# First three groups of a gated recurrence and its two-layer network, ordered by pairs

## The chip, the cores and the metric

The kernel runs on one core of one Trainium2 chip. The metric is device time in microseconds (us) for one execution, and the median over the runs is compared. Engines are named as in the profile: PE is TensorE (PEld its weight loads), DVE is VectorE, ACT is ScalarE, POOL is GpSimd, SP is SyncE, which here only issues DMAs.

## The reference

Four inputs q, k, v, alpha of shape (4 batches, 8 heads, 768 steps, 48 features) go through a recurrence with a state of 48 x 48 per batch and head. Its result, as 3072 tokens of 384 features, goes through a layer of 2048 units with GELU and a second layer back to 384.

```python
for t in range(S):
    state = alpha[:, :, t, :, None] * state + einsum('bhd,bhe->bhde', k[:, :, t], v[:, :, t])
    y[:, :, t] = einsum('bhd,bhde->bhe', q[:, :, t], state)
x = y.transpose(0, 2, 1, 3).reshape(B * S, H * D)        # 3072 x 384
h = x @ w_in                                             # 384 x 2048
g = gelu_tanh(h)
out = g @ w_out                                          # 2048 x 384
```

## The kernel before

**Tiles and groups.** The 768 steps are cut into six chunks of 128. A group G0 to G5 is one chunk of all four batches, four tiles of 128 tokens; a pair is two tiles of a group. Pairs are called p0 and p1 (G0), p2 and p3 (G1), p4 and p5 (G2).

**One pair through the recurrence.** ACT takes Ln of alpha (`e_ln`, L121). PE makes running sums over the chunk (`e_cum`, L129, and the chunk's total, L131). ACT takes three exponentials of them (`e_exp`: b, L142; its inverse, L143; the total, L144), and DVE multiplies q and k by the first two (qp, L146; kp, L148). Then for each tile: `t_qk` transposes qp and kp on PE (L165) and copies them out of PSUM (L167; on ACT where `evict` is `nc.scalar.copy`, else on DVE); `attn` makes the scores (PE, L178) and masks them (two DVE operations, L181); `kv` makes the chunk's contribution to the state (PE, L192) and updates the state (DVE, L201 and L203; in G0 L203 alone); `y` makes the output from old state and masked scores (PE, L214 and L217; in G0 L217 alone) and ACT copies it out (x, L220). x is transposed into xT either by PE and a DVE copy (`t_x`, L229 and L230) or by a DMA from SP (L222).

**The two layers.** `layer1` is a list of 16 pieces, each three PE products (L239) and one GELU on ACT (L242). For a half group a piece is 256 columns wide, for a whole group 512. `layer2` is a list of pieces of four products (L254), four pieces to a tile; the last of a tile is followed by a DVE copy (ot, L258) and a DMA out from SP.

**PSUM.** Three names share the eight banks: `ca` (two banks, one buffer, for the sums and for the scores of one tile), `yk` (two buffers: transposes, kv, y and xT) and `ff` (four buffers: pieces of layer 1, sums of layer 2).

**What sets the order.** The order is written out by hand: each engine does its work in the order in which `run` issues it. `_merge(main, side, first, last)` spreads a list of side work between the pieces of a list of main work. ACT holds one set of function tables at a time: `act_set(LN_EXP_SET)` (L112) loads one with Ln and Exp; before an activation whose function is not in the set that is loaded, the build puts a load of its own, listed under the line of that activation (L121, L142, L242).

**Order before.** p0 goes through whole (L325 to L328), then eight pieces of layer 1 for its half group, p1 whole, and the rest of layer 1 for G0. Layer 2 of G0 is merged with p2 (L341, L342). Layer 1 of the first half of G1 is merged with Ln, Exp and scores of p3 in its last 30% (L343, L344). Layer 2 of that half is merged with the state of p3 and with Ln and Exp of p4 and p5 (L346, L347), layer 1 of the second half with the scores of p4 and p5. From G2 on a loop (L352) does a group at a time: layer 2 of the group before, merged with the state of this group, its xT by DMA, and Ln and Exp of the next group; then layer 1 (512 columns wide), merged with the scores of the next group.

**Loads.** POOL issues all loads but the first, in the order of the program: G0 by pairs, between them the weights, then G1 by pairs, then G2 whole. a, q and k have two buffers each, so that a load for G2 waits until G0's has been used, and G3's until G1's has.

## Time and profile before

| | us |
|---|---|
| median of 3 runs (lowest to highest) | 240.38 (239.75 to 241.97) |
| the profiled execution, whole | 241.77 |
| its span, first to last instruction | 240.0 |
| PE busy | 186.0 (78%) |
| ACT busy | 134.3 (56%) |
| DVE busy | 108.7 (45%) |
| POOL busy | 51.5 (21%) |

The mean clock granted to TensorE over the span is 0.927 of full speed. Times in the profile are counted from the start of the span. A row of the timeline gives start, duration, engine, line, operation, result and sources, count, and in brackets the idle time before it and what ended it. A row of a table by stretches gives, after the stretch and its length, the busy time of PE, PEld, DVE, ACT and POOL with the number of instructions in parentheses, the granted clock, the share of DMA and GB/s. A busy PE is not a PE at its peak, since its products are pipelined.

### The profile page before, as it was taken

The page shows a single profiled execution, that of the slowest core. Times are in us where ns is not written, and L with a number is a line of the kernel's source. Part 1 is how long each engine was busy: PE and PEld are TensorE (multiplying, and loading weights), DVE is VectorE, ACT ScalarE, POOL GpSimd, SP SyncE. Part 2 cuts the span into 40 slices and gives each one's busy share as a digit, 9 for nine tenths or more (in the row PEclk, how much of TensorE's full clock was granted, in tenths as well). Part 3 has the DMA queues.
Part 4 walks back from the last instruction along what each step waited for, and adds up shares of the span by engine and source line. Part 5 has one row for each costly group of instructions (what it writes and reads, how often), then busy time and mean ns, then how long its engine had stood idle before and what let it go on. Part 6 is the DMA issues. An engine that isn't in the chain of part 4 may idle for free.

```text
span 240.0 us, 3997 instructions
## 1 busy us (share of the span) xinstructions
PE 186.0 (78%) x1641; PEld 116.0 (48%) x1648; DVE 108.7 (45%) x213; ACT 134.3 (56%) x228; POOL 51.5 (21%) x47
## 2 busy tenths in 40 slices
PE   0368258997665387569946999899998999999992
PEld 0146136864444155347622556554565555654561
DVE  5361234004750267377890465866568565110020
ACT  3426736944239926986851567486764865219600
POOL 7965634322000370162216000000000000000000
PEclk9999855999979559999995899999999999999999
DMA  7999999999900199979999961320012200240011
GB/s 144 174 214 178 203 216 175 172 190 181 163 33 0 31 192 182 89 163 209 145 169 216 169 21 37 80 85 3 0 52 66 82 3 0 68 112 19 0 68 67
DMA packets 44339, 26.22 MB, mean 109 GB/s; under 512 B 34304, under 2 KB 40960, under 8 KB 44320
## 3 DMA queue, kind: packets, MB, share of 16 engines
q0 software_dynamic: 32144, 19.27, 61.9%
q1 hardware_dynamic: 12176, 6.69, 11.5%
q8 instruction: 13, 0.21, 0.4%
q14 instruction: 6, 0.05, 0.1%
HBM read 25.17 MB, written 4.72 MB: 125 GB/s over the span
## 4 chain that ended last, share of the span: by engine, by line
PE 59%; DVE 13%; ACT 13%; DMA 7%; issue 5%; POOL 1%; DVEq 0%; POOLq 0%; ACTq 0%
PE hT L239 25%; PE acc L254 21%; PE qkT_ps L165 5%; PE at L178 4%; DMA xT<-x 3%; DVE atm L181 3%; DVE kp L148 3%; DMA k<-in_k_dram 3%; DVE qkT L167 2%; DVE st L203 2%; ACT gT L242 2%; ACT b L142 2%; ACT qkT L167 2%; ACT L142 2%; ACT L121 2%
## 5 line engine op out<-in xcount | busy, mean ns | idle before, releaser
L239 PE MATMUL hT<-xT,w_in 128*128 128x256 bf16 (+1 forms) x377 | 76.3, 352 | 8.1 <-DMA xT<-x 4.2
L242 ACT ACTIVATE gT<-hT 128x256 bf16<-128x256 f32 (+1 forms) x128 | 60.0, 491 | 32.2 <-PE hT L239 30.2
L254 PE MATMUL acc<-w_out,gT 128*128 128x384 bf16 x384 | 68.3, 326 | 0.0
L239 PEld LDWEIGHTS <-w_in 128*128 128x128 bf16 x384 | 38.8, 106 | 33.1 <-issue 6.9
L254 PEld LDWEIGHTS <-gT 128*128 128x128 bf16 x384 | 35.0, 97 | 21.3
L181 DVE TENSOR_TENSOR atm<-at,ut 128x512 bf16<-128x512 f32 x48 | 30.9, 686 | 23.8 <-PE at L178 23.8
L146 DVE TENSOR_TENSOR qp<-q,b 128x768 bf16<-128x768 f32 x12 | 11.5, 958 | 46.2 <-ACT b L142 45.7
L220 ACT CAST x<-yps 128x384 bf16<-128x384 f32 x24 | 11.5, 479 | 32.9 <-PE yps L217 25.3
L258 DVE COPY ot<-acc 128x384 f32<-128x384 f32 x24 | 13.4, 557 | 34.6 <-PE acc L254 33.1
L129 PE MATMUL cum<-la,ut_h 128*128 128x384 f16 x24 | 7.7, 350 | 16.4 <-ACT la L121 16.4
L91 POOL DMA_DIRECT2D a<-in_alpha_dram x7 | 10.2, 1458 | 47.1 <-ACT la L121 41.6
L167 DVE COPY qkT<-qkT_ps 128x1024 bf16<-128x1024 bf16 x18 | 12.4, 690 | 16.7 <-PE qkT_ps L165 16.7
L178 PE MATMUL at<-qkT 64*128 64x128 bf16 x192 | 10.7, 239 | 7.0 <-ACT qkT L167 4.9
L165 PE MATMUL qkT_ps<-ident,qp 128*128 128x128 bf16 x96 | 10.9, 245 | 6.5 <-DVE qp L146 6.5
L142 ACT ACTIVATE b<-cum 128x768 bf16<-128x768 f32 x12 | 9.7, 811 | 8.9 <-PE cum L131 7.6
L91 POOL DMA_DIRECT2D q<-in_q_dram x8 | 11.5, 1436 | 12.7 <-DVE qp L146 9.2
L91 POOL DMA_DIRECT2D v<-in_v_dram x8 | 11.4, 1428 | 11.1 <-issue 4.7
L178 PEld LDWEIGHTS <-qkT 64*128 64x128 bf16 x192 | 6.1, 102 | 15.8 <-ACT qkT L167 6.6
L165 PEld LDWEIGHTS <-qp 128*128 128x128 bf16 x96 | 7.9, 109 | 11.4 <-DVE qp L146 7.5
L131 PEld LDWEIGHTS <-la 128*128 128x128 f16 x96 | 5.6, 100 | 16.1 <-issue 11.9
L242 ACT ACT_TABLE_LOAD x9 | 11.5, 1283 | 2.5 <-PE hT L239 2.4
L165 PE MATMUL qkT_ps<-ident,kp 128*128 128x128 bf16 x96 | 10.9, 246 | 2.2 <-DVE kp L148 2.2
(40 smaller groups left out, 168.8 us busy)
## 6 DMA issues: line engine op xcount, KB each, us to landing
out_dram<-ot SPq DMA_DIRECT2D x24, 192.0 KB, 2.0
a<-in_alpha_dram POOLq DMA_DIRECT2D x4, 768.0 KB, 9.1
q<-in_q_dram POOLq DMA_DIRECT2D x4, 768.0 KB, 9.7
k<-in_k_dram POOLq DMA_DIRECT2D x4, 768.0 KB, 13.0
q<-in_q_dram POOLq DMA_DIRECT2D x4, 384.0 KB, 12.6
k<-in_k_dram POOLq DMA_DIRECT2D x4, 384.0 KB, 13.4
w_in<-in_moe_w_in_dram POOLq DMA_DIRECT2D x4, 384.0 KB, 9.4
w_out<-in_moe_w_out_dram POOLq DMA_DIRECT2D x4, 384.0 KB, 14.5
```

The lines of the kernel that those rows point to most:

```text
L91: (eng or self.nc.gpsimd).dma_start(t[:, lo:hi].rearrange("t b h d -> t (b h) d"), src)
L142: nc.scalar.activation(b8, cum[:, :, 0:H * D], AF.Exp)
L146: nc.vector.tensor_tensor(qp[:, :, :, 0:D], u0["qpair"], b8.rearrange("t i (h d) -> t i h d", h=H), op=ALU.mult)
L165: nc.tensor.transpose(ps[:, j, p, :], s[:, 2 * p:2 * p + 2, :].rearrange("t h d -> t (h d)"), self.ident)
L167: (evict or nc.vector.tensor_copy)(t, ps)
L178: nc.tensor.matmul(at[:, o, p, :], kT[sl, p, :], qT[sl, p, :], start=True, stop=True)
L181: nc.vector.tensor_tensor(atm[:, o], at[:, o], self.ut[:, None, :].to_broadcast([C, H // 2, C]), op=ALU.mult)
L220: nc.scalar.copy(x, yps.rearrange("t h d -> t (h d)"))
L239: nc.tensor.matmul(h, self.w_in[:, j, nt * C:(nt + 1) * C], xT[:, j, lo:hi].rearrange("p g t -> p (g t)"), start=j == 0, stop=j == self.NK ...
L242: nc.scalar.activation(gT[:, nt, lo * C:hi * C], h, AF.Gelu_apprx_tanh)
L254: nc.tensor.matmul(acc[mt], gT[:, nt, mt * C:(mt + 1) * C], self.w_out[:, nt, :], start=nt == 0, stop=nt == self.NFT - 1)
L258: nc.vector.tensor_copy(ot, acc[mt])
```

## The change

The order of work up to the end of layer 1 of G2 is written anew; the loop now begins at G3.

- G2 too is done in halves: p4 and p5 each have their own layer 1 and xT by PE and DVE instead of a DMA.
- A function `chain` takes a pair from transposes to xT: both transposes first, one copied out by DVE and one by ACT, then score and kv of the first tile, of the second tile, and the two outputs; `fill(i)` puts other work at five places. For p0 the fill is `warm(n)`: n products of zeros, 512 columns wide. For p1 it is layer 1 of p0's half group, for p2 pieces of layer 2 of G0.
- `decays` gives two steps, the first with the table load and Ln, the second with sums and exponentials. No GELU is issued between the two steps of a pair.
- p3, p4 and p5 have their scores merged into layer 1 of the half group before, and state, xT and decays of the next pair lie between pieces of layer 2.
- The loop is entered with eleven of the sixteen pieces of layer 2 of G2 left, and with the scores of G3 done.
- a, q and k get three buffers, the rings for la, qp and kp four, ot six; G2 is loaded by pairs, and the loads of G3 are issued behind layer 2 of G1. A tile of zeros is filled on DVE.

```diff
--- before.py
+++ after.py
@@ -60,12 +60,13 @@
         self.ut = const.tile([C, C], BF16, name="ut")
         self.ident = const.tile([C, C], BF16, name="ident")
         self.ones = const.tile([C, 1], F16, name="ones")
+        self.zero = const.tile([C, 512], BF16, name="zero")
 
         self.w_in = const.tile([C, self.NKT, self.d_ff], BF16, name="w_in")
         self.w_out = const.tile([C, self.NFT, self.d_model], BF16, name="w_out")
         self.state = [[const.tile([C, H // 2, 2 * D], BF16, name=f"st{b}_{i}") for i in range(2)]
                       for b in range(B)]
-        self.NR = 3
+        self.NR = 4
         self.la_ring = [const.tile([C, 2, H, 64], F16, name=f"la{i}") for i in range(self.NR)]
         self.qp_ring = [const.tile([C, 2, H, 64], BF16, name=f"qp{i}") for i in range(self.NR)]
         self.kp_ring = [const.tile([C, 2, H, 64], BF16, name=f"kp{i}") for i in range(self.NR)]
@@ -84,7 +85,7 @@
         c = group[0][0]
         if (n, c) not in self.loaded:
             self.loaded[n, c] = self.ld.tile([C, len(group), H, D], BF16 if n == "v" else F32, tag=n,
-                                             bufs=3 if n == "v" else 2, name=n)
+                                             bufs=3, name=n)
         t = self.loaded[n, c]
         lo, hi = (0, len(group)) if part is None else (2 * part, 2 * part + 2)
         src = self.src[n][lo:hi].rearrange("b h s d -> s (b h) d")[c * C:(c + 1) * C]
@@ -232,16 +233,31 @@
 
     def layer1(self, xT, gT, lo=0, hi=4):
         nc, C = self.nc, self.C
-
-        def piece(nt):
-            h = self.ps.tile([C, (hi - lo) * C], F32, tag="ff", bufs=4, name="hT")
+        hs = {}
+
+        def mm(nt):
+            h = hs[nt] = self.ps.tile([C, (hi - lo) * C], F32, tag="ff", bufs=4, name="hT")
             for j in range(self.NKT):
                 nc.tensor.matmul(h, self.w_in[:, j, nt * C:(nt + 1) * C],
                                  xT[:, j, lo:hi].rearrange("p g t -> p (g t)"),
                                  start=j == 0, stop=j == self.NKT - 1)
-            nc.scalar.activation(gT[:, nt, lo * C:hi * C], h, AF.Gelu_apprx_tanh)
-
-        return [lambda nt=nt: piece(nt) for nt in range(self.NFT)]
+
+        def act(nt):
+            nc.scalar.activation(gT[:, nt, lo * C:hi * C], hs.pop(nt), AF.Gelu_apprx_tanh)
+
+        def piece(nt):
+            mm(nt)
+            act(nt)
+
+        pieces = [lambda nt=nt: piece(nt) for nt in range(self.NFT)]
+        self.mm, self.act = mm, act
+        return pieces
+
+    def warm(self, n):
+
+        ps = self.ps.tile([self.C, 512], F32, tag="ff", bufs=4, name="idle")
+        for _ in range(n):
+            self.nc.tensor.matmul(ps, self.zero[:, 0:self.C], self.zero, start=True, stop=True)
 
     def layer2(self, group, gT, by_part=False, lo=0, hi=4):
         nc, C = self.nc, self.C
@@ -254,7 +270,7 @@
                 nc.tensor.matmul(acc[mt], gT[:, nt, mt * C:(mt + 1) * C], self.w_out[:, nt, :],
                                  start=nt == 0, stop=nt == self.NFT - 1)
             if part == self.NFT // 4 - 1:
-                ot = self.wk.tile([C, self.d_model], F32, tag="ot", name="ot")
+                ot = self.wk.tile([C, self.d_model], F32, tag="ot", bufs=6, name="ot")
                 nc.vector.tensor_copy(ot, acc[mt])
                 c, b = group[mt]
                 r = b * self.S + c * C
@@ -272,6 +288,7 @@
         pairs = [[g[0:2], g[2:4]] for g in G]
         self.act_set(LN_EXP_SET)
         self.load("a", G[0], 0, nc.sync)
+        nc.vector.memset(self.zero, 0.0)
         for n in "qkv":
             self.load(n, G[0], 0)
             if n == "q":
@@ -279,9 +296,8 @@
             if n == "k":
                 make_identity(nc, self.ident)
         nc.vector.memset(self.ones, 1.0)
-        self.pads(self.la_ring)
-        self.pads(self.qp_ring)
-        self.pads(self.kp_ring)
+        for i in range(self.NR):
+            self.pads((self.la_ring[i], self.qp_ring[i], self.kp_ring[i]))
         nc.vector.tensor_copy(self.ut, self.ut_h)
         for b in range(self.B):
             for i in range(2):
@@ -294,62 +310,102 @@
             self.load_w_in(i)
         for i in range(4):
             self.load_w_out(i)
-        for i in range(2):
-            for n in "aqkv":
-                self.load(n, G[1], i)
-        for n in "aqkv":
-            self.load(n, G[2])
-
-        def ln_exp(p):
-            self.e_ln(p)
-            self.e_cum(p)
-            self.e_exp(p)
-
-        def scores(p, evict=None):
-            return [f for cb in p for f in (lambda cb=cb: self.t_qk(cb, evict), lambda cb=cb: self.attn(cb))]
+        for g in (1, 2):
+            for i in range(2):
+                for n in "aqkv":
+                    self.load(n, G[g], i)
+
+        def run(*fs):
+            for f in fs:
+                f()
+
+        def decays(p):
+
+            return [lambda: (self.act_set(LN_EXP_SET), self.e_ln(p)), lambda: (self.e_cum(p), self.e_exp(p))]
+
+        def scores(p):
+            return [f for cb in p for f in (lambda cb=cb: self.t_qk(cb), lambda cb=cb: self.attn(cb))]
 
         def state(p, xT, lo):
-            for i, cb in enumerate(p):
-                self.yk(cb, xT, lo + i, False)
-            for i, cb in enumerate(p):
-                self.t_x(cb, xT, lo + i)
+            return [lambda i=i, cb=cb: self.yk(cb, xT, lo + i, False) for i, cb in enumerate(p)] + \
+                   [lambda i=i, cb=cb: self.t_x(cb, xT, lo + i) for i, cb in enumerate(p)]
 
         def new():
             return (self.grp.tile([self.C, self.NKT, 4, self.C], BF16, tag="xT", name="xT"),
                     self.grp.tile([self.C, self.NFT, 4 * self.C], BF16, tag="gT", bufs=1, name="gT"))
 
-        copy = nc.scalar.copy
-
-        (p0, p1), (p2, p3) = pairs[0], pairs[1]
+        def chain(p, xT, lo, fill):
+
+            u, w = p
+            fill(0)
+            self.t_qk(u)
+            self.t_qk(w, nc.scalar.copy)
+            fill(1)
+            self.attn(u)
+            self.kv(u)
+            self.attn(w)
+            self.kv(w)
+            fill(2)
+            self.y(u, xT, lo, False)
+            fill(3)
+            self.y(w, xT, lo + 1, False)
+            self.t_x(u, xT, lo)
+            fill(4)
+            self.t_x(w, xT, lo + 1)
+
+
+        p0, p1, p2, p3, p4, p5 = [p for g in (0, 1, 2) for p in pairs[g]]
         xT, gT = new()
-        ln_exp(p0)
-        for f in scores(p0, copy):
-            f()
-        state(p0, xT, 0)
-        first = self.layer1(xT, gT, 0, 2)
-        for f in first[:8]:
-            f()
+        self.e_ln(p0)
+        self.warm(10)
+        self.e_cum(p0)
+        self.e_exp(p0)
+        chain(p0, xT, 0, lambda i: self.warm((10, 3, 5, 2, 2)[i]))
         self.act_set(LN_EXP_SET)
-        ln_exp(p1)
-        for f in scores(p1, copy):
-            f()
-        state(p1, xT, 2)
-        for f in first[8:] + self.layer1(xT, gT, 2, 4):
-            f()
+        self.e_ln(p1)
+        la = self.layer1(xT, gT, 0, 2)
+        mm, act = self.mm, self.act
+        mm(0)
+        mm(1)
+        self.e_cum(p1)
+        self.e_exp(p1)
+        act(0)
+        act(1)
+        fill = {0: la[2:6], 1: la[6:8], 2: la[8:11], 3: la[11:13], 4: la[13:16]}
+        chain(p1, xT, 2, lambda i: run(*fill[i]))
+        run(*self.layer1(xT, gT, 2, 4))
+        l2 = self.layer2(G[0], gT, True)
         xT1, gT1 = new()
-        self.act_set(LN_EXP_SET)
-        side = [lambda: ln_exp(p2)] + scores(p2, copy) + [lambda: state(p2, xT1, 0)]
-        _merge(self.layer2(G[0], gT, True), side, 0.5, 1.0)
-        side = [lambda: self.act_set(LN_EXP_SET), lambda: ln_exp(p3)] + scores(p3)
-        _merge(self.layer1(xT1, gT1, 0, 2), side, 0.7, 1.0)
+        run(*l2[:4])
+        run(decays(p2)[0], *l2[4:6])
+        run(decays(p2)[1], *l2[6:11])
+        fill = {0: [], 1: l2[11:13], 2: l2[13:15], 3: l2[15:16], 4: []}
+        chain(p2, xT1, 0, lambda i: run(*fill[i]))
+        run(*decays(p3))
+        lc = self.layer1(xT1, gT1, 0, 2)
+        _merge(lc, scores(p3), 0.3, 0.9)
+        run(*state(p3, xT1, 2)[:2], decays(p4)[0])
         l2 = self.layer2(G[1], gT1, False, 0, 2)
-        side = [lambda: state(p3, xT1, 2)] + [lambda p=p: ln_exp(p) for p in pairs[2]]
-        _merge(l2, side, 0.1, 1.0)
-        side = [f for p in pairs[2] for f in scores(p)]
-        _merge(self.layer1(xT1, gT1, 2, 4), side, 0.1, 1.0)
-        prev = self.layer2(G[1], gT1, False, 2, 4)
-
-        for g in range(2, len(G)):
+        run(*l2[:1], *state(p3, xT1, 2)[2:], *l2[1:3], decays(p4)[1], *l2[3:])
+        _merge(self.layer1(xT1, gT1, 2, 4), scores(p4), 0.1, 0.9)
+        xT2, gT2 = new()
+        run(*state(p4, xT2, 0)[:2], decays(p5)[0])
+        l2 = self.layer2(G[1], gT1, False, 2, 4)
+        run(*l2[:1], *state(p4, xT2, 0)[2:], *l2[1:3], decays(p5)[1], *l2[3:])
+        self.load("a", G[3])
+        self.load("q", G[3])
+        self.load("k", G[3])
+        self.load("v", G[3])
+        _merge(self.layer1(xT2, gT2, 0, 2), scores(p5), 0.1, 0.9)
+        run(*state(p5, xT2, 2)[:2])
+        l2 = self.layer2(G[2], gT2, False, 0, 2)
+        (la0, ce0), (la1, ce1) = [decays(p) for p in pairs[3]]
+        run(la0, lambda: self.e_ln(pairs[3][1]))
+        run(*l2[:1], *state(p5, xT2, 2)[2:], *l2[1:2], ce0, *l2[2:5], ce1)
+        _merge(self.layer1(xT2, gT2, 2, 4), [f for p in pairs[3] for f in scores(p)], 0.1, 1.0)
+        prev = l2[5:] + self.layer2(G[2], gT2, False, 2, 4)
+
+        for g in range(3, len(G)):
             more = g + 1 < len(G)
             xT, gT = new()
```

## The prediction

> **What bounds the kernel now.** I read the busy time by stretches first, cut where a piece of layer work begins or ends on PE. The rows are: pair p0; p1 and the first layer of G0; second layer of G0 with p2; first layer of half of G1 with p3; from there to the end of the first layer of G2; the state of G2's successor beside G2's second layer; and the rest.
>
> ```profile
> 0.00:19.48 19.48, 6.92 (x73) 4.84 (x74) 9.69 (x31) 7.71 (x10) 15.29 (x23) 1.00 1.17 175
> 19.48:48.00 28.52, 20.46 (x168) 15.62 (x168) 6.45 (x12) 18.80 (x42) 12.75 (x12) 0.76 1.39 191
> 48.00:69.34 21.34, 15.32 (x146) 9.45 (x144) 9.81 (x20) 7.27 (x11) 3.24 (x2) 0.98 1.09 159
> 69.34:89.20 19.86, 11.92 (x91) 8.15 (x90) 4.50 (x6) 15.30 (x26) 5.42 (x4) 0.68 0.31 60
> 89.20:144.75 55.55, 42.99 (x432) 26.75 (x431) 33.97 (x62) 35.83 (x61) 14.77 (x9) 0.94 1.26 150
> 144.75:159.41 14.66, 13.91 (x152) 9.26 (x149) 11.85 (x25) 9.14 (x15) 0.00 (x0) 1.00 0.28 69
> 159.41:240.00 80.59, 74.52 (x593) 41.88 (x595) 32.38 (x58) 40.26 (x67) 0.00 (x0) 1.00 0.14 43
> ```
>
> The first number after the stretch is its length, the second PE's busy time. Behind 144.75 PE is busy over nine tenths of the time: PE bounds there, and the change leaves that code alone. Ahead of it PE idles for a quarter to two thirds, and the granted clock is partly halved. So what can be won lies in the first 145 us, in handovers. The timeline shows the worst one, ACT in the fourth stretch:
>
> ```profile
> 75.17 1.28 ACT L112 ACT_TABLE_LOAD   x1
> 76.46 1.28 ACT L242 ACT_TABLE_LOAD   x1
> 78.16 1.28 ACT L121 ACT_TABLE_LOAD   x1
> 80.31 1.28 ACT L142 ACT_TABLE_LOAD   x1
> 83.21 1.28 ACT L242 ACT_TABLE_LOAD   x1
> ```
>
> Five table loads in ten microseconds: a GELU stands between the explicit load and Ln, so Ln and then Exp load tables of their own. In the next stretch the state of G2 goes through xT by DMA, which PE waits for at its end:
>
> ```profile
> 128.03 0.59 PE L239 MATMUL hT<-xT,w_in 128*128 128x512 bf16 x1 [4.20 <-DMA xT<-x]
> ```
>
> **Are the loads early enough?** Issue rows, and the times to landing of those two:
>
> ```profile
> 9.76 1.17 POOL L91 DMA_DIRECT2D k<-in_k_dram  x1
> DMA to landing us min/median/max: 10.9/10.9/10.9
> 54.28 1.69 POOL L91 DMA_DIRECT2D v<-in_v_dram  x1 [4.73 <-issue]
> DMA to landing us min/median/max: 10.1/10.1/10.1
> ```
>
> k of p1 is there at 20.7, the last load of G2 at 64.4. Halving G2's loads moves the same bytes. Nothing but loads is queued on POOL, and third buffers only let G3's and G4's loads start sooner. The work below reaches p1's k at 21 and p5 after 83, so the loads cost nothing; with that cover gone, p1 would follow its k one for one.
>
> **Prices.** Of ACT and DVE, mean ns in the middle:
>
> ```profile
> L181 DVE TENSOR_TENSOR atm<-at,ut 128x512 bf16<-128x512 f32 x48 | 30.9, 686 | 23.8 <-PE at L178 23.8
> L167 DVE COPY qkT<-qkT_ps 128x1024 bf16<-128x1024 bf16 x18 | 12.4, 690 | 16.7 <-PE qkT_ps L165 16.7
> L201 DVE TENSOR_TENSOR stmp<-kv,st 64x192 f32<-64x192 f32 x32 | 11.3, 354 | 1.1 <-PE kv L192 0.6
> L258 DVE COPY ot<-acc 128x384 f32<-128x384 f32 x24 | 13.4, 557 | 34.6 <-PE acc L254 33.1
> L121 ACT ACTIVATE la<-a 128x768 f16<-128x768 f32 x12 | 10.1, 844 | 2.9 <-DMA a<-in_alpha_dram 2.8
> L220 ACT CAST x<-yps 128x384 bf16<-128x384 f32 x24 | 11.5, 479 | 32.9 <-PE yps L217 25.3 <-ACT la L121 3.0 <-DMA xT<-x 2.6
> ```
>
> Handovers, from the timeline:
>
> ```profile
> 27.89 0.81 ACT L142 ACTIVATE b<-cum 128x768 bf16<-128x768 f32 x1 [0.77 <-PE cum L131]
> 101.71 0.81 ACT L142 ACTIVATE b<-cum 128x768 bf16<-128x768 f32 x1
> 103.43 0.95 DVE L148 TENSOR_TENSOR kp<-k,binv 128x768 bf16<-128x768 f32 x1
> 104.61 0.66 ACT L242 ACTIVATE gT<-hT 128x256 bf16<-128x256 f32 x2
> 113.16 1.48 PE L254 MATMUL acc<-w_out,gT 128*128 128x384 bf16 x8
> 41.21 7.37 ACT L242 ACTIVATE gT<-hT 128x256 bf16<-128x256 f32 x22 [0.26 <-PE hT L239]
> 90.51 0.33 PE L192 MATMUL kv<-v,kp 128*128 128x96 bf16 x4
> 93.26 0.71 PE L229 MATMUL xT_ps<-ident,x 128*128 128x128 bf16 x6 [0.62 <-ACT x L220]
> ```
>
> So from the end of Ln to b 0.77 (PE's sums lie in it); from b to kp's end 2.67; from b to the first GELU, with its table load, 2.9; a half-group piece of layer 1 0.335 (7.37/22); a pair's state from kv to the transposes of x 2.75, the transposes 0.7. From the chain of waits, PE alone:
>
> ```profile
> 139.28 0.45 PE qkT_ps L165 x8
> 134.51 0.33 PE at L178 x8
> 204.08 1.95 PE acc L254 x12
> ```
>
> A tile's transposes 0.45, its scores 0.33, a piece of layer 2 0.65.
>
> **The change part by part.** Times are of the new kernel.
>
> p0: its start is set by k, as before:
>
> ```profile
> 9.42 0.96 DVE L148 TENSOR_TENSOR kp<-k,binv 128x768 bf16<-128x768 f32 x1 [0.84 <-DMA k<-in_k_dram]
> ```
>
> kp is done at 10.4. Transposes to 10.9; then DVE sets the pace: copy 0.69, scores and handover 0.4, masks 1.37, state 0.7 (two updates in G0), masks, state: 16.1. The last y, x, transposes and copy into xT add 0.4+0.5+0.4+0.4 and handovers, some 1.9 (y as kv's 0.33; the copy an estimate, half of 0.69): layer 1 can start at 18.0 (19.5 before). Copying the second tile on ACT hides beside the first tile's masks. The 22 products of zeros: 512 columns cost two thirds of a 0.335 piece, 0.22, or 0.45 at half clock. Ten end by 5.5 even so, ahead of Ln's end; ten lie in the wait for k; the rest beside DVE's masks. No row shows a product of zeros. Below: if they hold the clock, the chain runs as priced. Above: if they do nothing for it, PE's part of p0 doubles, the zeros included, and layer 1 starts near 23. Dense work earned the clock in every row I have, so I take the lower. The added fills on DVE lie ahead of kp, in a stretch where it is idle for half the time.
>
> p1: ACT is free at 17.1; table 1.28, Ln 0.84, 0.77: b at 20.0 and kp at 22.7. PE issues four pieces and the sums; the fifth piece waits for one of four PSUM buffers, until the first GELU ends at 23.3, and p1's transposes are queued behind the fifth and sixth: they end at 24.5, not 23.2. Copy 25.2; two pieces, scores 26.1; masks, state, masks, state 30.2; the tail with five pieces in it 32.6. The copies of x are queued on ACT behind up to three GELUs; that is in the tail. PE and ACT do the rest of the sixteen pieces beside DVE; without that cover they would cost their 0.335 each. Then 16 pieces at 0.335: layer 1 of G0 ends at 38.0 (48.0 before).
>
> p2: last GELU 38.4, table, Ln: 40.5; six pieces of layer 2 are done at 41.9; b at 42.6, kp 45.3; five more pieces and the sums to 45.8; transposes and copy 47.0; two pieces to 48.0. DVE now has 0.56 for ot, then masks 1.37, state 1.42, masks, state, three ot 1.7, xT 0.7: 56.6. p3's sums stand in PE's queue ahead of layer 1 of G1, so PE waits for x (54.8), table, Ln (56.9), then does four pieces and stops for the first GELU: b at 57.7, GELU at 60.6. Twelve pieces (4.0), two tiles' scores (1.6) and the refilling of the buffers: 67.0 (89.2 before). Here the ping-pong is gone; what is late next is this stop of 1.6.
>
> p4, p5: state 2.75 with a piece of layer 2 in its end, transposes 0.7, two pieces 1.3, to 72.1; ACT meanwhile has table and Ln done at the same time; sums 0.7, five pieces 3.25; the first GELU is possible 8.7 after the start, so hidden. Layer 1 with scores 5.4+1.6. One such cycle is 16.1: 83.1 and 99.2.
>
> G3's decays: state, pieces, transposes to 103.6; Ln at 104.3; sums 0.7; the second Ln (0.84) is queued before the first b at 105.1; three exponentials 1.6; b of the second pair waits for `ca` and starts at 107.5; first GELU 110.4. The same merge took from 104.61 to 113.16, 8.55: layer 1 of G2 ends at 119.0. The stretch from 89.20 before was 55.55, here 52.0, with five pieces of layer 2 done already and the wait for DMA gone: PE and DVE take over those four transposes (0.35 of PE per tile), and SP keeps only the stores, for which six buffers of ot leave DVE no wait.
>
> Loop entry: the stretch of 14.66 has 3.25 less of PE work. But DVE was busy for 11.85 of it, so between 11.9 and 14.7; with state and kp in series I take 13.5: 132.5. The rest as before, 80.6: 213.1.
>
> **The clock.** Windows of 3.41 us:
>
> ```profile
> 65.17:68.59 3.42, 1.15 (x18) 0.86 (x18) 3.15 (x9) 0.48 (x1) 0.00 (x0) 1.00 0.19 69
> 68.59:72.00 3.41, 2.69 (x14) 1.82 (x13) 0.67 (x3) 1.77 (x3) 0.00 (x0) 0.50 0.00 0
> 72.00:75.41 3.41, 3.06 (x28) 2.60 (x27) 0.00 (x0) 3.39 (x12) 0.00 (x0) 1.00 0.00 0
> 95.89:99.31 3.42, 1.85 (x19) 1.07 (x17) 1.79 (x2) 3.40 (x5) 0.00 (x0) 1.00 2.81 154
> 99.31:102.72 3.41, 2.27 (x26) 1.77 (x25) 0.20 (x2) 3.37 (x5) 1.68 (x1) 1.00 0.06 6
> ```
>
> PE busy for 1.15 of 3.42 lost the clock, 2.69 at half clock won it back, 1.85 at full clock kept it. My stops at p1 (20.7 to 23.3) and p3 (59 to 60.6, behind another wait) leave 0.8 to 1.7 in a window, as it falls. One loss doubles some seven pieces, 7 x 0.335 = 2.3. I add one: 215.5 of span. The Trainium skill ("TensorE: Matmul & The Clock Gate", HAM oscillation) has the clock lost by idle gaps over about 3.4 us; by that I would add nothing, 213.1, but the row with 1.15 lost it without such a gap.
>
> In the ping-pong rows one load follows another after 1.29, so a load costs 1.28 and nothing beside it. The Trainium skill ("ScalarE: Activation LUTs", What ACT_TABLE_LOAD costs) puts a switch at 2.66 with a drain; with eight loads on my path (two at p1, p3 and G3, one at p4 and p5) that would give 226.5, which the 1.29 speaks against.
>
> **The rivals.** A: zeros don't earn the clock, or short chains lose it repeatedly: p0 +5, p1 and p2 +2 each, 224.5. For it: 1.15 lost it. Against: fills leave few gaps.
> B: the change doesn't do what it says, and loads still part Ln from Exp: three more than needed for p3, as in the ping-pong rows, and as many for p4 and p5, 9 x 1.29 = 11.6: 227.1. Against it: in the code no GELU is issued between the two steps of a pair.
> C: handovers overlap better and no clock is lost: the 2.4, the stop at p3 and a 13.5 that is 11.9: 209.9. For it, masks overlap in pairs.
> D, slower than before: the clock, once lost near 20, stays at half until the loop, since no window is full enough. Of layer 1 some 90 half pieces, of layer 2 37 lie there; they cost 0.335 and 0.65 more each: 30+24, and with 213.1 that is 267. It decides from some 25 us of such work on (slower than 240 by the sum). Against it: 2.69 busy of 3.41 was followed by the full clock, and pure layer stretches of 5 us are left.
>
> **How the numbers follow.** The profiled execution was 241.77 for a span of 240.0; the median lies 1.39 below it. So 215.5 of span is 217.3 profiled and 215.9 in the median; I say 216. Chances: forecast (211 to 219) 0.70, A 0.12, B 0.03, C 0.10, D 0.05. The range 210 to 226 takes in A and most of C; B and D lie above it. One per cent is about what a measurement of this kernel can tell from no change. Faster by more 0.94, within 0.02 (the edge of D), slower 0.04.
>
> **What would show it.** Right: no loads under L121 and L142; layer 1 of G1 starting near 58, of G3 near 134; no wait for xT by DMA at G2. Wrong: clock 0.50 from 24 on; p1's transposes waiting for k; PE waiting for DVE for over 3 us in the loop's first stretch; a fifth piece not stopping at p1 and p3.

## The result, and the profile after

The changed kernel takes 215.69 us (median of four runs, 214.48 to 216.57); the kernel before, on the same chip, 241.07 (239.75 to 241.97). The ratio is 0.895, with a 95% interval of 0.888 to 0.902. The forecast was 216, with a range of 210 to 226. All ratios are formed from executions within 1.5% of the fastest of their kernel; one of the four without zeros and three of the six later ones of the changed kernel are longer, and count in the medians alone. The profiled execution is the shortest of the four: 214.48, with a span of 212.7 where the kernel before had 240.0.

The same seven stretches as in the prediction, each cut at the same event of the new kernel, the last at the start of G3's first layer (busy time by stretches; the numbers after the length are PE, PEld, DVE, ACT and POOL, then the granted clock):

```profile
0.00:18.04 18.04, 12.65 (x103) 6.26 (x105) 10.95 (x36) 6.50 (x9) 14.59 (x22) 1.00 1.13 178
18.04:37.47 19.43, 14.54 (x168) 12.20 (x168) 7.04 (x13) 15.61 (x40) 9.79 (x9) 1.00 1.33 199
37.47:56.56 19.09, 15.65 (x156) 10.01 (x154) 10.23 (x21) 8.39 (x12) 10.13 (x10) 0.97 1.42 186
56.56:65.76 9.20, 8.34 (x86) 6.46 (x84) 4.97 (x7) 7.55 (x19) 4.27 (x3) 0.87 1.30 231
65.76:117.60 51.84, 45.70 (x512) 33.35 (x510) 34.96 (x67) 37.02 (x79) 15.16 (x9) 1.00 1.22 171
117.60:132.03 14.43, 12.26 (x132) 7.97 (x129) 11.17 (x24) 8.60 (x14) 0.00 (x0) 0.88 0.22 57
132.03:212.70 80.67, 74.52 (x593) 41.88 (x595) 32.55 (x58) 40.38 (x67) 0.00 (x0) 1.00 0.14 42
```

The lengths before were 19.48, 28.52, 21.34, 19.86, 55.55, 14.66 and 80.59. So 1.4 us went in p0, 9.1 in p1 with layer 1 of G0, 2.3 in p2, 10.7 in the first layer of half of G1, 3.7 in the long stretch and 0.2 in the loop's first; the rest takes 0.1 longer. The two large terms are the two stages in which PE idled and the clock was partly halved.

The timeline of PE shows where each stage begins and what it waited for. The columns are start, duration, engine, line, tiles and shape, count, and in brackets the idle time before and what ended it:

```profile
18.04 0.81 PE L241 MATMUL hT<-xT,w_in 128*128 128x256 bf16 x6 [0.45 <-DVE xT L231]
23.43 0.82 PE L241 MATMUL hT<-xT,w_in 128*128 128x256 bf16 x6 [2.69 <-ACT gT L246]
32.23 5.40 PE L241 MATMUL hT<-xT,w_in 128*128 128x256 bf16 x48 [0.45 <-DVE xT L231]
56.56 2.64 PE L241 MATMUL hT<-xT,w_in 128*128 128x256 bf16 x12
60.07 0.81 PE L241 MATMUL hT<-xT,w_in 128*128 128x256 bf16 x6 [0.86 <-ACT gT L246]
67.03 0.33 PE L193 MATMUL kv<-v,kp 128*128 128x96 bf16 x4 [0.57 <-ACT x L221]
109.35 0.82 PE L241 MATMUL hT<-xT,w_in 128*128 128x256 bf16 x6 [1.68 <-ACT gT L246]
126.97 0.33 PE L215 MATMUL yps<-st,qkT 128*128 128x96 bf16 x4 [1.60 <-DVE stmp L202]
132.03 2.11 PE L241 MATMUL hT<-xT,w_in 128*128 128x512 bf16 x8
```

Three stops wait for the first GELU after a table load, at p1, p3 and G3, and p1's transposes come only behind the first of them, at 24.1, as the prediction had it. G2's first layer waits for no transfer. The stretch of ACT where five loads stood in ten microseconds is now this; Ln, both exponentials and GELU take two loads:

```profile
53.52 1.28 ACT L113 ACT_TABLE_LOAD   x1
54.82 0.84 ACT L122 ACTIVATE la<-a 128x768 f16<-128x768 f32 x1
56.74 0.81 ACT L143 ACTIVATE b<-cum 128x768 bf16<-128x768 f32 x1 [1.08 <-PE cum L132]
58.34 1.28 ACT L246 ACT_TABLE_LOAD   x1
59.63 1.76 ACT L246 ACTIVATE gT<-hT 128x256 bf16<-128x256 f32 x6
```

The clock still dips, but otherwise than forecast. The clock's two changes to half lie 71.67 us apart, 21 windows of 3.413; the boundaries of the other windows are counted from there. Of these four windows (columns as in the first fence) two were run at half clock, the only ones on the clock's record inside this run:

```profile
21.45:24.86 3.41, 1.43 (x20) 1.35 (x20) 1.45 (x3) 3.29 (x9) 2.48 (x3) 1.00 1.25 204
55.58:58.99 3.41, 3.28 (x22) 2.25 (x22) 1.41 (x2) 2.31 (x5) 1.68 (x1) 0.50 1.10 204
123.84:127.25 3.41, 1.24 (x30) 1.04 (x29) 3.30 (x7) 0.87 (x3) 0.00 (x0) 1.00 0.29 80
127.25:130.67 3.42, 3.42 (x28) 1.85 (x25) 1.58 (x6) 1.42 (x3) 0.00 (x0) 0.50 0.34 73
```

p1's stop did not lose the clock; the handover from p2 to p3 did, and so did the loop's first stretch, which the prediction had not listed. The experiments come back to this. One caution: the column shows 1.00 up to the first change on record, whatever the clock was. The first ten products of zeros took 3.89 us and the next ten 2.32, and in the kernel before four transposes of p0 took 0.61 where they take 0.40 here. So PE began slowly in both, and the 1.00 of p0 before, which the prediction's table has too, does not mean full clock.

### The profile page after: what moved, and what is told of

The parts are those of the page before. It is cut to its first block, busy times and chain, and to the rows that moved or that the text cites. A ratio compares the mean times of both kernels' runs of the same rounds, so it can differ in the third digit from the quotient of the medians.

```text
span 212.7 us, 4196 instructions
## 1 busy us (share of the span) xinstructions
PE 183.7 (86%) x1734; PEld 118.1 (56%) x1740; DVE 111.9 (53%) x224; ACT 124.0 (58%) x235; POOL 53.9 (25%) x51
## 4 chain that ended last, share of the span: by engine, by line
PE 50%; DMA 20%; POOL 8%; issue 8%; DVE 6%; ACT 6%; SPq 0%; POOLq 0%; ACTq 0%; DVEq 0%
PE acc L270 20%; PE hT L241 19%; DMA w_out<-in_moe_w_out_dram 7%; DMA a<-in_alpha_dram 7%; DMA q<-in_q_dram 5%; PE at L179 3%; PE qkT_ps L166 2%; POOL v L92 2%; DVE atm L182 2%; PE cum L130 2%; POOL q L92 2%; POOL a L92 2%; POOL k L92 2%; DVE qkT L168 2%; DMA xT<-x 1%
## 5 line engine op out<-in xcount | busy, mean ns | idle before, releaser
L241 PE MATMUL hT<-xT,w_in 128*128 128x256 bf16 (+1 forms) x427 | 71.7, 311 | 8.0 <-ACT gT L246 5.6
L246 ACT ACTIVATE gT<-hT 128x256 bf16<-128x256 f32 (+1 forms) x144 | 60.7, 457 | 24.1 <-PE hT L241 22.5
L241 PEld LDWEIGHTS <-w_in 128*128 128x128 bf16 x432 | 40.4, 99 | 27.4 <-issue 9.2
L274 DVE COPY ot<-acc 128x384 f32<-128x384 f32 x24 | 13.2, 556 | 33.2 <-PE acc L270 32.8
L221 ACT CAST x<-yps 128x384 bf16<-128x384 f32 x24 | 11.5, 478 | 29.0 <-PE yps L218 26.6
L147 DVE TENSOR_TENSOR qp<-q,b 128x768 bf16<-128x768 f32 x12 | 11.5, 958 | 27.3 <-ACT b L143 27.1
L168 DVE COPY qkT<-qkT_ps 128x1024 bf16<-128x1024 bf16 x21 | 14.5, 691 | 15.1 <-PE qkT_ps L166 15.1
L92 POOL DMA_DIRECT2D k<-in_k_dram x9 | 12.0, 1331 | 7.9 <-DVE stmp L202 3.9
L179 PE MATMUL at<-qkT 64*128 64x128 bf16 x192 | 9.5, 218 | 4.7 <-DVE atm L182 3.7
L113 ACT ACT_TABLE_LOAD x9 | 11.5, 1283 | 0.9 <-PEq L448 0.7
L149 DVE TENSOR_TENSOR kp<-k,binv 128x768 bf16<-128x768 f32 x12 | 11.4, 952 | 1.2 <-DMA k<-in_k_dram 1.2
L204 DVE TENSOR_TENSOR st<-stmp,bend 64x192 bf16<-64x192 f32 x32 | 11.3, 353 | 1.4
L122 ACT ACTIVATE la<-a 128x768 f16<-128x768 f32 x12 | 10.0, 842 | 2.9 <-DMA a<-in_alpha_dram 2.8
L202 DVE TENSOR_TENSOR stmp<-kv,st 64x192 f32<-64x192 f32 x32 | 11.3, 353 | 0.5
## 6 DMA issues: line engine op xcount, KB each, us to landing
k<-in_k_dram POOLq DMA_DIRECT2D x6, 384.0 KB, 13.3
```

The lines of the kernel that those rows point to most:

```text
L92: (eng or self.nc.gpsimd).dma_start(t[:, lo:hi].rearrange("t b h d -> t (b h) d"), src)
L113: nc.scalar.add_instruction(mybir.InstLoadActFuncSet(name=nc.get_next_instruction_name(), act_func_set_id=i, engine=mybir.EngineType.Activ ...
L147: nc.vector.tensor_tensor(qp[:, :, :, 0:D], u0["qpair"], b8.rearrange("t i (h d) -> t i h d", h=H), op=ALU.mult)
L149: nc.vector.tensor_tensor(kp[:, :, :, 0:D], u0["kpair"], binv8.rearrange("t i (h d) -> t i h d", h=H), op=ALU.mult)
L168: (evict or nc.vector.tensor_copy)(t, ps)
L179: nc.tensor.matmul(at[:, o, p, :], kT[sl, p, :], qT[sl, p, :], start=True, stop=True)
```

## The experiments

Theory for all of them: the gain is the sum of idle time taken out of stages, above all p1 (filled with layer work) and p3 (Ln and Exp kept together); loads, third buffers and zeros change little. Rivals are named with each run. The first four runs share one chip and their executions of the kernel before (median 241.62); so do the three one-step orders and the zeros in the loop (240.05, one execution), and the other four (241.63). Parts of a run are compared by stretches. A run with one time only was executed once.

**The zeros taken out** of the changed kernel:

```diff
-        self.warm(10)
...
-        chain(p0, xT, 0, lambda i: self.warm((10, 3, 5, 2, 2)[i]))
+        chain(p0, xT, 0, lambda i: None)
```

> The changed kernel without the 22 products of zeros, else the same. My theory: they earn the full clock ahead of p0, and without them PE does p0 at half clock, but DVE and ACT set the pace of that chain, so layer 1 of G0 starts only 0.5 to 1 us later (18.5 to 19.0 instead of 18.04); p1's first pieces and sums are at half clock too, the clock comes back between 22 and 28, and the span is 1 to 3 us longer (213.7 to 215.7). Rival: zeros do nothing for the clock, or the chain is set by DVE and ACT alone: the start stays within 0.2 us and the span within 0.5 us of 212.7. Second rival, the prediction's upper bound: start at 23, span 217 or more.

Measured: 215.32 us (213.96 to 217.49), ratio to the kernel before 0.890 [0.887, 0.894]. Timeline of PE:

```profile
17.85 1.44 PE L241 MATMUL hT<-xT,w_in 128*128 128x256 bf16 x6 [0.45 <-DVE xT L231]
33.65 5.40 PE L241 MATMUL hT<-xT,w_in 128*128 128x256 bf16 x48 [0.45 <-DVE xT L231]
```

Without zeros PE is at half clock (1.44 for six products, against 0.81), and yet layer 1 starts at 17.85, no later than 18.04. That is the rival's 0.2 and not the 0.5 to 1 later that was expected. So in p0 the clock does not matter: DVE's masks and copies set the pace. In p1 the second half of layer 1 starts 1.42 earlier in the first profiled run, with zeros and full clock, than here. But of the nine traced runs that have the zeros and this order of p1, seven lose the clock there all the same, as the windows fall, and start that half at 33.2 to 35.8. So the runs show no lasting gain from these zeros, and the medians, 215.3 without and 215.7 with them, show none either.

**Two buffers for a, q and k** instead of three:

```diff
-                                              bufs=3, name=n)
+                                              bufs=3 if n == "v" else 2, name=n)
```

> The changed kernel with two buffers for a, q and k, as before the change. My theory: the loads are far ahead and the third buffers cost nothing and bring nothing: layer 1 of G3 starts within 0.5 us of 132, span within 1 us of 212.7. Rival: part of the gain is from loads that come earlier; G3's loads would wait for p3 again, G4's for p5 and G5's for G3, and would lie beside the DMAs into xT in the loop's first stretch, whose 4.2 us of waiting before the change would come back there: span 215 to 217.

Measured: 216.65, span 214.9, more than the 1 us around 212.7 that was expected. But the difference of 2.2 to the first profiled run is not the loads'. PE's timeline and, below it, two windows of the clock:

```profile
33.46 0.81 PE L241 MATMUL hT<-xT,w_in 128*128 128x256 bf16 x6 [0.45 <-DVE xT L231]
69.89 0.33 PE L193 MATMUL kv<-v,kp 128*128 128x96 bf16 x4 [0.57 <-ACT x L221]
```

```profile
20.76:24.17 3.41, 0.93 (x11) 0.86 (x11) 1.91 (x2) 3.38 (x9) 2.27 (x2) 1.00 1.31 202
24.17:27.58 3.41, 3.41 (x32) 2.54 (x29) 0.88 (x2) 2.06 (x5) 2.34 (x3) 0.50 1.31 202
```

The stop at p1 has the same length, 2.69, and ends at 23.2. But here nearly all of it lies within one window, PE is busy for 0.93 of 3.41, and the next window runs at half clock: 1.23 lost by 33.46. Another 1.6 goes at p3, where two windows are lost rather than one, and from 69.89 on the distance to the first profiled run stays at 2.9, until the last wait for xT by DMA, near 190, which is 0.5 here and 1.2 there. Behind p0 no wait for a load appears, on PE, ACT or DVE. So in this trace the third buffers are worth nothing, as was said.

**Ln and Exp together, alone.** The kernel before, with only the order of p3's and G2's decays changed, and p3's scores spread over layer 1 from 30% to 90%:

```diff
-        side = [lambda: self.act_set(LN_EXP_SET), lambda: ln_exp(p3)] + scores(p3)
-        _merge(self.layer1(xT1, gT1, 0, 2), side, 0.7, 1.0)
+        ln_exp(p3)
+        _merge(self.layer1(xT1, gT1, 0, 2), scores(p3), 0.3, 0.9)
...
-        side = [lambda: state(p3, xT1, 2)] + [lambda p=p: ln_exp(p) for p in pairs[2]]
+        side = [lambda: state(p3, xT1, 2), lambda: self.act_set(LN_EXP_SET)] + [lambda p=p: ln_exp(p) for p in pairs[2]]
```

> The kernel before with one part of the change: Ln and Exp of p3 ahead of layer 1 of G1's first half, its scores merged into that layer, and one table load ahead of Ln and Exp of p4 and p5. My theory: the stretch from 69.34 to 89.20 shrinks to some 9.5 us as in the changed kernel, and the next one loses three table loads of 1.28, so 13 to 14 us in all: span 226 to 228, time near 227. Rival: the gain is given back later, because G3's and G4's loads or the DMAs into xT end the next wait: span over 233.

Measured: 228.78 us (228.29 to 229.47), ratio 0.948 [0.945, 0.952], span 226.7. PE's timeline:

```profile
78.49 1.46 PE L254 MATMUL acc<-w_out,gT 128*128 128x384 bf16 x8
115.75 3.75 PE L239 MATMUL hT<-xT,w_in 128*128 128x512 bf16 x9 [4.39 <-DMA xT<-x]
```

Layer 1 of G1 starts where it did before (69.29 against 69.34) and ends 10.7 earlier (78.49 against 89.20). From there to the end of G1's first layer another 1.8 is won (22.2 against 24.0), and 1.0 in layer 1 of G2, where one window runs at half clock and not two; the whole span is 13.3 shorter. Nothing later takes it back; the wait for xT by DMA is still there. So three changed lines of order are worth half of the whole change. They do two things at once: 14 table loads are left of 22, 10.3 us less on ACT, and p3's decays come ahead of layer 1 instead of in its last 30%. What each of the two is worth alone was not measured.

**The first group alone.** The kernel before, with p0 and p1 (and the zeros) of the changed one, everything from p2 on in the old order:

```diff
+        self.e_ln(p0)
+        self.warm(10)
...
+        chain(p0, xT, 0, lambda i: self.warm((10, 3, 5, 2, 2)[i]))
...
+        fill = {0: la[2:6], 1: la[6:8], 2: la[8:11], 3: la[11:13], 4: la[13:16]}
+        chain(p1, xT, 2, lambda i: run(*fill[i]))
+        run(*self.layer1(xT, gT, 2, 4))
```

> The kernel before with the other part alone: p0 and p1 as in the changed kernel (products of zeros, the chain, layer 1 of p0's half group filled into p1), all from the second layer of G0 on as before. My theory: layer 2 of G0 starts at 37.5 instead of 48.0 and the 10.5 us stay: span 229 to 230. Rival: the loads bound what follows (the last of G2 lands at 64), or a lost clock takes it back: span over 234. Together with the tables alone, additive parts leave some 2 to 4 us of the 27 to the order of p2, p4, p5 and the halves of G2.

Measured: 237.84 us (236.20 to 239.35), ratio 0.986 [0.980, 0.991], span 234.4, where 229 to 230 was expected. Layer 2 of G0 starts at 37.39, 10.6 earlier than before, as expected; but layer 1 of G1 only 5.3 earlier. The rest was given back by a wait that neither theory had named. Timeline, all engines:

```profile
59.35 0.56 DVE L274 COPY ot<-acc 128x384 f32<-128x384 f32 x1 [6.14 <-DMA out_dram<-ot]
61.04 0.48 PE L215 MATMUL yps<-st,qkT 128*128 128x96 bf16 x4 [6.74 <-DVE stmp L202]
64.01 2.22 PE L241 MATMUL hT<-xT,w_in 128*128 128x256 bf16 x10 [0.45 <-DVE xT L231]
```

DVE's fourth output copy waits 6.14 for one of three buffers of `ot`, that is for a store to land, and DVE's state updates for p2 are queued behind it, so PE waits 6.74. For the stores of this kernel the trace gives "1.8/2.0/10.1" us from issue to landing (shortest, median, longest): the first three, issued between 50.5 and 53.2 while G2 is loaded, took 8.5 to 10.1, the fourth 4.3.

**The same with six buffers of `ot`** takes that wait away and leaves all else:

```diff
-                ot = self.wk.tile([C, self.d_model], F32, tag="ot", name="ot")
+                ot = self.wk.tile([C, self.d_model], F32, tag="ot", bufs=6, name="ot")
```

> The kernel before with p0 and p1 as in the changed kernel (the earlier run, span 234.4) and six buffers for ot. My theory: the 5 us that were given back there lie in one wait of DVE, 6.14 for a store at the fourth copy; with six buffers it goes, layer 1 of G1 starts near 58.3 instead of 64.0, and the span is 228.5 to 230. Rival: the wait only moves on to the loads or to table loads, and the span stays over 232.

Measured: 230.30, span 228.5. PE's timeline:

```profile
58.46 1.47 PE L241 MATMUL hT<-xT,w_in 128*128 128x256 bf16 x12 [0.63 <-DVE xT L231]
```

Layer 1 of G1 starts 5.6 earlier than with three buffers, although this run lost the clock once in p1, and DVE waits for no store. So what the first group gave back was this one wait. With the store's wait gone, the first group takes 11.5 off the span of before (240.0), and Ln with Exp 13.3. Each was run alone; added up they are 24.8 of the 27.3. The remaining 2.5 was not taken apart; the wait for xT by DMA (4.2 before) lies in it, against smaller stops.

**Three buffers of `ot` in the changed kernel** ask whether the new order needs the six:

```diff
-                ot = self.wk.tile([C, self.d_model], F32, tag="ot", bufs=6, name="ot")
+                ot = self.wk.tile([C, self.d_model], F32, tag="ot", name="ot")
```

> The changed kernel with three buffers for ot, as before the change, where DVE's fourth copy of layer 2 of G0 has to wait for the first store. My theory: the store lands 8 to 9 us after its issue beside the loads (issue 48.1), so the copy waits until 56.7 instead of running at 54.5, and with it the copies into xT behind it: layer 1 of G1 starts 1.5 to 2.5 us later. Rival, the prediction's price: nothing, the wait of 1.3 in the kernel before is hidden.

Measured: 216.23, span 214.5. Timeline:

```profile
59.24 0.56 DVE L274 COPY ot<-acc 128x384 f32<-128x384 f32 x1 [1.16 <-DMA out_dram<-ot]
60.38 2.72 PE L241 MATMUL hT<-xT,w_in 128*128 128x256 bf16 x12 [0.47 <-DVE xT L231]
```

The wait is there, but 1.16 long, and only 0.47 of it reaches PE. That is less than expected. The run lost three windows in a row in p1 (its second half of layer 1 starts at 35.76), so the loads were further on when its stores began, and at the usual pace the wait may be longer; that was not measured.

**Three stops taken away by order.** First p1, two pieces less ahead of the transposes, so that the fifth piece comes behind them:

```diff
-        fill = {0: la[2:6], 1: la[6:8], 2: la[8:11], 3: la[11:13], 4: la[13:16]}
+        fill = {0: la[2:4], 1: la[4:6], 2: la[6:10], 3: la[10:13], 4: la[13:16]}
```

> The changed kernel with p1's transposes ahead of the fifth piece of layer 1 instead of behind the sixth; the pieces move into later places of the chain. My theory: the stop at the fifth piece, for the first GELU, holds up the transposes by 1.3 us and is on the path: they start at 22.8 instead of 24.09, layer 1 of G0's second half starts near 31.0 instead of 32.23, span near 211.5. Rival: ACT sets this stretch (GELUs and copies), and the start of the second half stays within 0.3 us of 32.2.

Measured: 214.21, span 212.4. PE's timeline:

```profile
22.88 0.40 PE L166 MATMUL qkT_ps<-ident,kp 128*128 128x128 bf16 x4 [0.47 <-DVE kp L149]
31.33 0.92 PE L241 MATMUL hT<-xT,w_in 128*128 128x256 bf16 x7 [0.45 <-DVE xT L231]
```

The transposes now wait for kp, 1.2 before the time at which they were held up behind the GELU, and the second half of layer 1 starts 0.9 earlier than in the changed kernel. So the stop was on the path, as the prediction's step for p1 says. The span shows only 0.3 of it, because this run lost two windows of clock at p3 (55.6 to 62.4).

Second p3: its Ln put ahead of p2's state instead of behind it.

```diff
-            run(decays(p2)[1], *l2[6:11])
+            run(decays(p2)[1], lambda: self.e_ln(p3), *l2[6:11])
...
-            run(*decays(p3))
+            run(decays(p3)[1])
```

> The changed kernel with Ln of p3 right behind the exponentials of p2, so that no table load and no Ln stand between p2 and p3's sums. My theory: the handover from p2 to p3 is bound by table load, Ln, sums, exponentials and GELU's table on ACT, so the first GELU of G1 comes at 57.5 instead of 59.63, the clock is not lost there (no 0.50 near 56), and the span is 2.1 us shorter, near 210.6. Rival: xT and DVE bind there too, and less than 1 us is won.

Measured: 213.31, span 211.5. PE's timeline:

```profile
53.31 0.81 PE L270 MATMUL acc<-w_out,gT 128*128 128x384 bf16 x4
57.28 1.47 PE L241 MATMUL hT<-xT,w_in 128*128 128x256 bf16 x12 [0.89 <-DVE xT L231]
59.75 0.81 PE L241 MATMUL hT<-xT,w_in 128*128 128x256 bf16 x6 [1.00 <-ACT gT L246]
```

This run lost the clock in p1 and came to the last piece of layer 2 at 53.31, 1.68 later than the changed kernel's first profiled run (51.63). From there to the end of the stop it takes 6.44, against 8.44 (60.07 less 51.63): 2.0 won. PE's wait of 1.81 for Ln ahead of the sums is gone, and the clock is not lost here. The order alone is worth 1.7 of it: a later run of the unchanged text, with the full clock over p3's sums, takes 8.11 (53.03 to 61.14).

Third G3's decays: Ln of both pairs behind the exponentials of p5, ahead of layer 1 of G2's first half, and for that the loads of G3 issued ahead of G1's last pieces of layer 2.

```diff
...
+        run(*[lambda p=p: self.e_ln(p) for p in pairs[3]])
...
-        run(la0, lambda: self.e_ln(pairs[3][1]))
+        run(lambda: self.act_set(LN_EXP_SET))
```

> The changed kernel with Ln of both pairs of G3 behind the exponentials of p5, their loads issued earlier, and only the table load left in the state of p5. My theory: ACT binds from there to the first GELU; it comes 0.8 us earlier (108.1 instead of 108.91), span near 211.9. Rival: the two Ln delay the first GELU of layer 1 of G2 near 92.3, and nothing or less is won.

Measured: 215.77, span 214.0, with the clock lost in p1, twice at p3 and once in the loop. Against the run of the unchanged text that lost the same windows (next but one), PE resumes after the stop at 111.28 instead of 112.32, 1.0 earlier, and the next stretch begins 1.04 earlier:

```profile
111.28 0.81 PE L241 MATMUL hT<-xT,w_in 128*128 128x256 bf16 x6 [1.68 <-ACT gT L246]
119.53 1.64 PE L270 MATMUL acc<-w_out,gT 128*128 128x384 bf16 x9
```

**Zeros where the loop loses the clock**: six of them between kv and y of G3's last tile.

```diff
-                side += [lambda: self.yk(G[g][3], xT, 3), ...
+                if g == 3:
+                    side += [lambda: (self.kv(G[g][3]), self.warm(6), self.y(G[g][3], xT, 3, True))]
...
```

> The changed kernel with six products of zeros between kv and y of the last tile in the loop's first stretch, where PE waits 1.6 us for DVE and then runs at half clock (0.50 from 127.3 to 130.7). My theory: products of zeros count as work for the clock: it stays at 1.00, and layer 1 of G3 starts 0.8 to 1.2 us earlier, 130.9 instead of 131.9. Rival: zeros don't count: the clock is lost at the same place and nothing changes, or the zeros delay y.

Measured: 216.00, span 214.2, with the clock lost in p1 and twice at p3. The later run of the unchanged text (next) came to this stretch at the same time, 120.57, and its windows fall alike; so the two differ in the zeros alone. Here are its windows, then those with the zeros, then the timeline with them:

```profile
126.50:129.90 3.40, 1.27 (x23) 0.95 (x22) 3.32 (x6) 1.18 (x3) 0.00 (x0) 1.00 0.19 47
129.90:133.30 3.40, 3.35 (x28) 1.99 (x28) 1.77 (x5) 0.89 (x2) 0.00 (x0) 0.50 0.43 107
```

```profile
126.47:129.88 3.41, 2.54 (x28) 1.51 (x28) 3.33 (x6) 1.21 (x3) 0.00 (x0) 1.00 0.21 48
129.88:133.30 3.42, 3.36 (x38) 2.22 (x37) 2.57 (x7) 2.09 (x5) 0.00 (x0) 1.00 0.42 105
```

```profile
120.57 2.12 PE L270 MATMUL acc<-w_out,gT 128*128 128x384 bf16 x12
133.82 1.46 PE L241 MATMUL hT<-xT,w_in 128*128 128x512 bf16 x6 [0.21 <-DMA xT<-x]
```

With the zeros PE is busy for 2.54 of the first window instead of 1.27, and the second one keeps the full clock. From the first piece of layer 2 to layer 1 of G3 it takes 13.25, against 14.38 in that run (134.95 less 120.57) and 14.43 in the first profiled one: 1.1 to 1.2 won. What is late next is a transfer, by 0.21.

**The changed kernel again**, beside the next one on one chip:

> The changed kernel again, beside the next one on the same chip. My theory: its time depends on where the clock's windows of 3.41 us fall: a window that holds p1's whole stop (20.7 to 23.4) loses the clock, which costs 1.2 to 1.6 us there, and a second lost window at p3 another 1.4; so 214.5 to 217, median 215 to 216.

Measured: 216.47 us, six runs from 213.57 to 218.24; the median is above the 215 to 216 that was expected. The ratio to the kernel before is 0.890 [0.886, 0.894]. The profiled execution is the longest of them. Two windows of it, and the two rows that give the distance to the first profiled run:

```profile
20.70:24.10 3.40, 0.81 (x9) 0.74 (x9) 1.83 (x2) 3.37 (x9) 2.32 (x2) 1.00 1.28 202
24.10:27.50 3.40, 3.40 (x32) 2.55 (x29) 0.69 (x1) 2.19 (x5) 2.30 (x2) 0.50 1.31 203
```

```profile
33.63 1.58 PE L241 MATMUL hT<-xT,w_in 128*128 128x256 bf16 x13 [0.45 <-DVE xT L231]
120.57 2.12 PE L270 MATMUL acc<-w_out,gT 128*128 128x384 bf16 x12
```

The same program, 1.4 later at 33.63 and 3.0 later at 120.57. Up to there the instructions are the same and wait for the same things; what differs is where the boundaries of the clock's windows fall. The stop at p1 runs from 20.6 to 23.3 here and from 20.7 to 23.4 there. Here a window runs from 20.7 to 24.1 and holds nearly nothing else. In the first profiled run a boundary at 21.45 cut it in two, and the window behind it had 1.43 of busy time and kept the clock. This run lost four windows, one at p1, two at p3 and one in the loop. Its span ends 3.7 later than the first one's: the other 0.8 is the wait for xT near 190, 2.0 here and 1.2 there.

Executions without a trace have their mean granted clock on record. One window at half clock takes 0.008 off it (half of 3.41, of some 214). In the ten executions of the unchanged text two windows (0.984) go with spans of 211.8 and 212.7, three (0.976) with 213.2 to 214.4, and four (0.966 to 0.968) with 214.8 to 216.4. So a lost window costs about 1.5 on average in the untraced executions too, and with the wait near 190 that makes up most of the spread; which windows each of them lost is not on record.

**All four together**, the three orders and the zeros in the loop:

> The changed kernel with four edits together: p1's transposes ahead of the fifth piece, Ln of p3 and of G3 early, products of zeros in the loop's first stretch. Measured apart, by stretches, they gave 0.9, 2.0, 1.0 and 1.2 us, and the first two also leave the clock nothing to lose at p1 and p3. My theory: they add, 5 us against a run of the changed kernel without a lost clock at p1 (span near 207.6) and up to 7 against one with it; time near 209.5, ratio to the kernel before 0.865 to 0.875. Rival: what is won early is given back in the loop's first stretch or to the loads: span over 210.

Measured: 210.23 us (208.93 to 211.69, six runs), ratio to the kernel before 0.871 [0.867, 0.874], where the changed kernel had 0.890 on the same chip. It is faster than both kernels. Layer 1 of G3, which started at 132.03 in the changed kernel's first profiled run, starts 4.0 earlier, and waits only for a transfer:

```profile
128.06 2.10 PE L241 MATMUL hT<-xT,w_in 128*128 128x512 bf16 x9 [0.28 <-DMA xT<-x]
```

The single steps gave 0.9, 2.0, 1.0 and 1.1 to 1.2, in all 5.0 to 5.1. The profiled run lost one window, at p1, and none at p3 or in the loop; for that window its second half of layer 1 started at 32.32, and not at 31.33 as in the first step's run. Without this 1.0 the start of layer 1 of G3 would be 5.0 earlier, so the steps add. The medians differ by 6.2 and the ratios by 0.019, some 4.6 us. These hold the clock as well: 0.984 to 0.996 in the six executions here, 0.966 to 0.984 in those of the changed kernel.

## Why the prediction was right, step by step

**What bounds it.** Right. All of the gain but 0.2 lies ahead of the loop, in the handovers; the rest took 80.7 against 80.6 said.

**Loads.** Right: no load is waited for in the new places, and taking the third buffers away brought no wait for one. The changed kernel's chain of waits seems to say otherwise, since 20% of it is DMA in the first profiled run. That chain is followed back through whatever released an instruction last, and loads that ran far ahead can stand in it: in the later run of the same text 4% of it is DMA, and with two buffers 4% as well.

**p0.** 18.0 said, 18.04 measured. The rival inside this step was wrong in its size: the upper bound of 23 assumed that PE at half clock, zeros included, would set p0's pace. Without zeros, at half clock, it starts at 17.85. The value taken was right, for another reason than the one given (dense work earning the clock): the clock does not enter it.

**p1.** The fifth piece stopped as said, for a GELU that came at 23.4 (23.3 said); the second half of layer 1 started at 32.2 (32.6), layer 2 at 37.5 (38.0). The run with the other order confirms that the stop, and not kp, held the transposes.

**p2 and p3.** Layer 1 of G1 started at 56.6 (57.7 said), the first GELU came at 59.6 (60.6), and the stage ended at 65.8 (67.0). The chain was right, link by link; the handovers in p2 were counted about 1 us too long in all. That Ln and Exp together were the larger of the two parts, 13.3 against 11.5, is shown by the runs that did only one of them.

**p4, p5, G3.** From 65.76 to 117.60 it took 51.84, and 52.0 was said; the stop at G3 is there. The wait for xT by DMA is gone.

**Output buffers.** Said to leave DVE no wait, which holds. Not said was how much hung on it: with three, stores that land 8.5 to 10.1 us after their issue cost 5.6 in the old order of p2. In the new order it cost 0.5 in the one run that shows it.

**Loop entry.** 13.5 said, and 14.43 measured to layer 1 of G3. The 0.9 is the clock (13.25 with the zeros, which keep it): the step had the work right and did not see that this stretch loses a window. The sign to look for, a wait for DVE of over 3 us, did not come; it was 1.60.

**The clock.** This step had the kind of loss right, but neither its places nor its size. One loss at 2.3 was added. The first profiled run lost two windows, at p3 and at the loop's entry. The one at p3 cost about 0.3: the later run of the same program had the full clock over p3's sums, and its distance to the first shrank from 1.40 to 1.08 there (57.64 against 56.56); the half-speed pieces behind the sums lie in the wait for the first GELU. The one at the loop cost 1.2. Other profiled runs lost one at p1 for 1.2 to 1.7 and two at p3 for some 1.5 more. So each loss is smaller than 2.3, and the profiled runs of the unchanged text had two and four of them: 1.5 in all in the first, 4.4 in the later one (1.4, 0.3 and 1.5, and 1.2), with the 2.4 of the forecast between them.

**From span to median.** The prediction put the median 1.4 below the profiled execution, because it had been so before. In the new kernel the profiled execution was the shortest, 1.2 below the median, so this step was 2.6 too low. The forecast for the profiled execution itself, 217.3, was 2.8 too long: the work without lost clock came to about 211.2 of span (212.7 less 1.2 and 0.3) where 213.1 was said, 1.9 less, and the clock took 1.5 where 2.4 was allowed. That 216 lies within 0.3 of the median is luck: errors of 2.8 and 2.6 met. The size of the gain is not luck; either error alone would have left the time well inside the range.

**Rivals.** A (zeros don't hold the clock) fell in p0, but its second half, short chains losing the clock repeatedly, is partly true, at 1.5 to 4.4 in the two profiled runs of the unchanged text. B fell: no load remains under Ln's or Exp's line. Nine stand under the explicit one, and seven under GELU's:

```profile
L113 ACT ACT_TABLE_LOAD x9 | 11.5, 1283 | 0.9 <-PEq L448 0.7
```

C came about in half: the handovers were shorter, but clock was lost. D fell: the later run did show its sign, 0.50 from 24.1 on, but for one window; in the changed kernel half clock never lasted beyond two windows (three with three buffers of `ot`), and no run was near 240.

## What to carry to other kernels

Keep the functions of one table set together, and look at what an engine's queue holds behind an instruction that must wait: here one order (Ln with Exp, ahead of the layer) was worth 13 us, one output buffer that came back late 5.6, and moving work ahead of a stop 1 to 2 each. Before you trust a saved stage, look for the next thing that is shared with it; stores that run beside loads come back late. Where a lost clock moves the total by several microseconds, compare kernels stretch by stretch, between the same two events and among runs that lost the same windows.

## What the runs showed of the hardware

The clock is decided window by window, and the windows' boundaries are not tied to the program. One and the same stop of 2.7 us lost the clock where it lay within a window (busy 0.81 and 0.93 of 3.41) and not where a boundary cut it (1.43). The Trainium skill ("TensorE: Matmul & The Clock Gate", The HAM clock gate) calls the window of 3413 ns free-running, and the runs agree. Its rule in the same place, that the clock is lost after an idle window of that length, read as a window without any work, is not what these windows show: 0.81 to 1.27 us of work in a window was not enough, and PE's longest wait beside them was 2.69. The bound cannot be said more closely by busy time as modelled, since 1.43 stands in a window that kept the clock and also in this one that lost it:

```profile
52.17:55.58 3.41, 1.43 (x20) 0.86 (x19) 3.26 (x9) 2.71 (x4) 0.82 (x1) 1.00 1.65 212
```

At p3 in the later run 1.52 lost it too, while 1.67 around the stop of G3 kept it. Once at half clock, a window with 2.10 busy did not win it back there; full ones did, and 2.69 did in the kernel before.

Products of zeros count as work for the clock: six of them raised a window from 1.27 to 2.54 busy, and it kept the full clock. In p0 nothing hung on them.

A table load took 1.28 us, and the next ACT instruction began 1.29 to 1.30 after the load's start (53.52 to 54.82, 58.34 to 59.63): nothing came on top of it.

A store of 192 KB took 8.5 to 10.1 us to land beside the loads of G2; of the twenty stores behind 90 us in the same run the median was 1.9 and the longest 7.2.
